# Turned probabilities loaded into every fourth partition, and x loaded ahead of two weight groups

## The chip, the cores and the metric

The kernel runs on one core of a Trainium2 chip. The metric is the time of one execution on the device, in microseconds (us). Five engines work side by side, each through its own instructions in order: TensorE (PE, with its weight loads shown apart as PEld), VectorE (DVE), ScalarE (ACT), GpSimd (POOL) and SyncE (SP). SP issues nearly all transfers here. A transfer is spread over 16 DMA engines; "DMA share" is the mean busy share of these.

## The reference, cut to what matters

```
# attention with a forget gate: 4 batches, 8 heads, 576 positions, head size 64
scores = q @ k.T / sqrt(64) + (cum_i - cum_j)       # cum = cumsum(log(clip(f)))
attn   = softmax(causal(scores));  attn_out = attn @ v
x  = attn_out as (2304 tokens, 512)
h  = maximum(x @ w1_in, 0);        x = (h * h) @ w1_out      # first MLP, 512 -> 2048 -> 512
h  = x @ w2_in;  g = h - tanh(h);  out = g @ w2_out          # second MLP
```

All of it is float32. The kernel gets float32 accuracy out of faster matmuls by splitting an operand into a high and a low part (names ending in h and l, or hi and lo) and adding three products.

## The kernel before, in words

There are 32 units, one for each batch and head. The 8 units of batch 0 are done first; units 8 to 31 then run beside the first MLP, whose matmuls (L159 for `h_step`, L175 for `y_step`) work on tiles of 288 tokens and stand between the attention's matmuls on PE. The MLP of token tile j needs the attention output of these tokens, which goes through the DRAM tensor `x_d` (`store_x`, then `load_x`).

A unit's probabilities `P` stand with queries in the partitions; the product with V wants keys in the partitions. Units 8 to 15 turn them on PE (`trans`). Units 16 to 31 (`UT = 16`) turn them differently: DVE transposes 32x32 blocks into the tile `T` (`turn`), `put` stores T (1 MB) into the DRAM tensor `p_d`, and `get` loads it into the tile `PTl` with four transfers of 256 KB, one for each block b of 32 keys, each into 32 partitions with four runs of 2 KB in a partition. Then POOL rounds `PTl` to `PTh` (`split_p`, L108), DVE leaves the rest in `PTl` (L119), and `pv` multiplies both with V: seven matmuls with 128 rows of weights and 512 to 256 columns (L561), one with the last 64 keys (L558) and one with the first query tile's 64 keys (L563). V comes from `load_v` (tile `VR`), with key 128c + p in partition p.

`T`, `PTl` and `PTh` have one buffer each, so a unit's `get` waits for the product of the unit before, and a unit's first transposition waits for `put` of the unit before. In the loop `attention_late` the pieces of unit k stand between those of unit k - 1 (`split_p`, `pv`); `get(k)` is emitted last.

What sets the order: from MLP tile 2 on (`MARK`) until tile 6, the order of each engine's instructions is chosen when the kernel is built, by a scheduler that works with its own durations of instructions and transfers. Before and after this stretch the order is that of the code.

The second part is the second MLP. `w_load(0, g)` loads the prepared weights of group g (two transfers of 896 KB into tile `wg`), `x_load(b)` the 576 tokens of block b (two transfers of 576 KB into `xa`), and the loop over n makes the steps of 42 matmuls each, eight steps for a token block. Step n works with weight group `HSEQ[n % 8]`, in the order 6, 7, 0, 1, 2, 3, 4, 5; groups 6 and 7 are in place already. In step 3 of a block, `x_op` (ACT, then POOL) begins to split the next block's x. `h_store` stores a step's result `gq` into `g_d`, from SP like the loads.

Of the kernel before, what the change touches and what calls it, by code (L numbers as in the profile page):

```python
# [9 lines left out]
F32 = mybir.dt.float32  # L10
# [22 lines left out]
UT = 16  # L33
# [32 lines left out]
def kernel(  # L66
# [10 lines left out]
    nc = tc.nc  # L77
# [107 lines left out]
    R, QA, QB, VR, VH, ST, XS, P, PT = {}, {}, {}, {}, {}, {}, {}, {}, {}  # L185
# [65 lines left out]

    def load_v(u):
        VR[u] = two.tile([128, 5, D], F32, tag="VR", bufs=2, name="VR")
        nc.sync.dma_start(VR[u], v[u])

    def prep_v(u):
        VH[u] = one.tile([128, 4, 2, D], F32R, tag="VH", name="VH")
# [251 lines left out]
    def turn(t):  # L509
        p, T = P[t], PT["t"]  # L510
        if t == 0:
            nc.vector.transpose(T[0:64, 0:2, 3, 0], p[0:64, :64].rearrange("p (b j) -> p b j", b=2))
            return
        nch = min(t + 1, 4)
        nc.vector.transpose(T[:, :, :nch, t - 1].rearrange("p b a j -> p a b j"),
                            p[:, :nch * 128].rearrange("p (a b j) -> p a b j", a=nch, b=4))
        if t == 4:
            nc.vector.transpose(T[:, 0:2, 2, 0], p[:, 512:576].rearrange("p (b j) -> p b j", b=2))
# [4 lines left out]
    def get(u):  # L523
        src = p_d[u % 2].rearrange("(q i) (b n) -> i q b n", q=4, b=4)
        for b in range(4):
            dst = PT["l"][32 * b:32 * b + 32].rearrange("p q a s j -> p q (a s j)")
            by("get").dma_start(dst.bitcast(F32), src[:, :, b])  # L527

    def split_p(a):
# [6 lines left out]
    def pv(u):  # L536
        vh, vr = VH.pop(u), VR.pop(u)
        b, h = divmod(u, H)
        e = h % 2
        ps = bank(u, "o_ps")  # L540
        if u < UT:
            hi, lo = (PT[k].rearrange("p q a s j -> p (q a s j)").rearrange("p (c t j) -> p c t j", c=4, t=4) for k in "hl")
            po = ps.rearrange("p (s j) -> p s j", s=4)
            at = lambda p, c, t: p[:, c, t:]
            po4, p4 = ps[0:64, 384:512].rearrange("p (q j) -> p q j", q=4), PT["t"][0:64, :, 3, 1]
            po_at = lambda t: po[:, t:]
            p0 = PT["t"][0:64, 2:4, 3, 0]
        else:
            hi, lo = PT["h"], PT["l"]
            po = ps.rearrange("p (q s j) -> p q s j", q=4, s=4)  # L550
            at = lambda p, c, t: p[:, :, c, t:]
            po4, p4 = po[0:64, :, 3], lo[0:64, :, 2, 0].bitcast(F32)
            po_at = lambda t: po[:, :, t:]
            p0 = lo[0:64, 0:2, 3, 0].bitcast(F32)
        seq = [(hi, 0), (hi, 1), (lo, 1), (hi, 2), (lo, 2), (hi, 3), (lo, 3), (None, 4), (lo, 0)]
        for n, (pt, c) in enumerate(seq):
            if pt is None:
                nc.tensor.matmul(po4, vr[0:64, 4], p4, start=False, stop=False)  # L558
                continue
            t = max(0, c - 1)  # L560
            nc.tensor.matmul(po_at(t), vh[:, c].rearrange("p a d -> p (a d)"), at(pt, c, t), start=(n == 0), stop=(n == 8))  # L561
        ps0 = bank(u, "o0_ps")
        nc.tensor.matmul(ps0[0:64, 0:64], vr[0:64, 0], p0, start=True, stop=True)  # L563
        if e == 0:
            XS[0] = two.tile([128, S], F32, tag="xs", name="xs")
        xs = XS[0]
        r = slice(64 * e, 64 * e + 64)
        xt = one.tile([64, 512], F32, tag="xsh", name="xt")
        rounded(nc.scalar, xt, ps[64:128])
        if u < UT:  # L570
            nc.vector.tensor_tensor(xs[r, 64:], ps[0:64], xt, ALU.add)
        else:
            nc.vector.tensor_tensor(
                xs[r, 64:].rearrange("p (s q j) -> p q s j", s=4, q=4),
                ps[0:64].rearrange("p (q s j) -> p q s j", q=4, s=4),
                xt.rearrange("p (q s j) -> p q s j", q=4, s=4), ALU.add,
            )
        rounded(by(pre(u) + "xs0"), xs[r, 0:64], ps0[0:64, 0:64])
        if e == 1:
            store_x(b, h // 2, xs, 0, S)  # L580
# [11 lines left out]
    def attention(u0):  # L592
        for p in range(u0 - 2, UT):
            if u0 - 1 <= p:
                load_v(p + 1)
            for t in (1, 4, 3, 2):
                if p >= u0:
                    trans(p, t)
                    yield
                if u0 <= p + 1:  # L600
                    scores(p + 1, t)
                    if t == 1:
                        scores(p + 1, 0)
                    elif p + 1 == UT:
                        turn(t)
                    yield
                if t == 4 and p + 2 < NU:
                    prep(p + 2)
                if t == 3 and p >= u0:
                    prep_v(p)  # L610
            if p + 3 < NU:
                load(p + 3)
            if p >= u0:
                pv(p)
            if p + 1 == UT:
                turn(1)
                turn(0)
                put(UT)
                get(UT)
            if p >= u0:  # L620
                yield
# [261 lines left out]
    def w_load(s, g):  # L883
        hl = home(s, g)
        for a in range(2):
            nc.sync.dma_start(hl[:, a].bitcast(F32), wg_d[s][g][:, a, s:])
        place(s, g, hl)
# [45 lines left out]
    for g in range(NB * NF + LAG):  # L933
        j, i = divmod(g, NF)
        if (j, i) == MARK:
            first_part = {x.name for x in nc.cur_bb.bb.instructions}
        if j < NB:
# [16 lines left out]
            if j < len(PACE):  # L954
                lo, hi, end = PACE[j]
# [195 lines left out]
    for n in range(NSTEP):  # L1151
        b, g = divmod(n, NG)
        x = [bank2(*RING7[(3 * n + i) % 7])[:, :N2] for i in range(3)]
        BK[n] = [x[0], bank2(0, 0)[:, :N2], x[1], x[2]]
        cp, uv, xc, c22 = (SM[:, 2 * i + n % 2] for i in range(4))
        if n < 3:
            w_load(0, n + 3)
        if g == XLOAD_AT and b + 1 < B:
            x_load(b + 1)
        if n in YGT_AT:  # L1160
            y_load(YGT_AT[n])
        if g == 1 and b:
            x_op(b, ("B22",))

        for p in ("P6", "P1", "P7", "P5"):
            h_prod(n, p)
        nc.scalar.activation(cp, BK[n][0], AF.Copy)
        nc.vector.tensor_tensor(uv, BK[n][1], cp, ALU.add)
        now, end = parts(n)
        for k, a in now:  # L1170
            split_part(k, a)
        for k, a in now:
            for which in range(2):
                prep_store(1, k, which, a, a + 4)
        if b + 1 < B and g in XOP_AT:
            x_op(b + 1, XOP_AT[g])
        if b and g in XOP_NEXT:
            x_op(b, XOP_NEXT[g])
        nc.vector.tensor_tensor(BK[n][2], BK[n][2], uv, ALU.add)
        nc.scalar.activation(xc, BK[n][2], AF.Copy)  # L1180
        if g == NG - 1 and b + 1 < B:
            x_op(b + 1, ("T3",))
        nc.vector.tensor_tensor(c22, BK[n][3], xc, ALU.add)
        nc.vector.tensor_tensor(BK[n][3], BK[n][3], uv, ALU.add)
        if g == NG - 1 and b + 1 < B:
            x_op(b + 1, ("T1",))
        if n in YHI_AT and n == NSTEP - 1:
            y_hi(YHI_AT[n])
        if n:
            GQ[n - 1] = late.tile([128, 4, N2], F32, tag="gq", bufs=2, name="gq")  # L1190
            for k in (0, 3, 1, 2):
                h_rest(n - 1, k)
        if g in TSUM_AT and b + 1 < B:
            x_sum(b + 1, TSUM_AT[g])
        for k in at_step(n, -2):
            raw_wide(k, 0)
        for k in at_step(n, -1):
            raw_wide(k, 1)
        for k in at_step(n, 0):
            for m in range(2):  # L1200
                raw_or(k, m)
            if k + 1 < NG:
                prep_fetch(1, k + 1)
        for d, names in ((1, ("S1", "S3")), (2, ("S2", "S4"))):
            for k in at_step(n, d):
                for name in names:
                    prep_sum(1, k, name)
        for k in at_step(n, -1):
            for m in range(2):
                raw_shift(k, m)  # L1210
        for k, a in end:
            split_part(k, a)
        if n in YSUM_AT:
            y_sum(YSUM_AT[n])
        if n in YHI_AT and n < NSTEP - 1:
            y_hi(YHI_AT[n])
        if n == NSTEP - 2:
            y_lo(0)
        if n:
            h_store(n - 1)  # L1220
        for k, a in end:
            for which in range(2):
                prep_store(1, k, which, a, a + 4)
        if n in YLOAD_AT:
            w_load(1, YLOAD_AT[n])

    n = NSTEP - 1
# [116 lines left out]
```

## Time and profile before

| what | value |
|---|---|
| median of 3 runs | 1060.38 us (1056.74 to 1061.86) |
| the profiled execution: its time | 1054.99 us |
| the profiled execution: its span | 1053.2 us |
| PE busy | 992.8 us (94% of the span) |
| DVE, ACT, POOL busy | 71%, 56%, 38% |
| moved by DMA | 211.55 MB, mean 201 GB/s |

The span runs from the first to the last instruction; the execution's time is 1.8 us longer. All times of instructions below are counted from the span's start. A line number is that of the kernel before. In the profile an idle time stands in front of the instruction that ended it, with what released it behind an arrow.

### The profile page before, as it was taken

The page shows a single profiled execution, that of the slowest core. Times are in us where ns is not written, and L with a number is a line of the kernel's source. Part 1 is how long each engine was busy: PE and PEld are TensorE (multiplying, and loading weights), DVE is VectorE, ACT ScalarE, POOL GpSimd, SP SyncE. Part 2 cuts the span into 40 slices and gives each one's busy share as a digit, 9 for nine tenths or more (in the row PEclk, how much of TensorE's full clock was granted, in tenths as well). Part 3 has the DMA queues.
Part 4 walks back from the last instruction along what each step waited for, and adds up shares of the span by engine and source line. Part 5 has one row for each costly group of instructions (what it writes and reads, how often), then busy time and mean ns, then how long its engine had stood idle before and what let it go on. Part 6 is the DMA issues. An engine that isn't in the chain of part 4 may idle for free.

```text
span 1053.2 us, 19722 instructions
## 1 busy us (share of the span) xinstructions
PE 992.8 (94%) x7008; PEld 927.2 (88%) x7008; DVE 743.7 (71%) x1843; ACT 587.7 (56%) x1314; POOL 400.3 (38%) x484
## 2 busy tenths in 40 slices
PE   4989999999998989898999999979999999999998
PEld 3667678888987979888889999969999999999998
DVE  5897777777876777677733667548787788877851
ACT  5886777665464655545445777526565663333330
POOL 4244455554444344443310555416474630000000
PEclk9999999999998999999999999989999999999999
DMA  8657642224955746755634987786868599535442
GB/s 243 198 151 208 195 153 98 83 82 152 295 165 159 226 159 217 222 139 193 192 97 144 339 320 245 274 320 228 298 241 297 195 352 373 165 95 160 141 147 74
DMA packets 86738, 211.55 MB, mean 201 GB/s; under 512 B 8592, under 2 KB 33232, under 8 KB 84336
## 3 DMA queue, kind: packets, MB, share of 16 engines
q1 hardware_dynamic: 86640, 210.29, 60.3%
q8 instruction: 55, 0.90, 0.4%
q14 instruction: 43, 0.35, 0.1%
HBM read 132.21 MB, written 78.05 MB: 200 GB/s over the span
## 4 chain that ended last, share of the span: by engine, by line
PE 60%; DVE 15%; DMA 15%; ACT 3%; issue 3%; SPq 2%; POOL 1%; POOLq 0%; DVEq 0%; ACTq 0%
PE wp L1085 15%; PE hp L159 11%; PE yp L175 11%; PE wp L1009 10%; DMA PTl<-p_d 6%; PE o_ps L561 3%; DMA p_d<-T 3%; PE wp L1097 2%; PE o_ps L376 2%; DVE PTl L119 2%; DVE P L452 2%; DMA g_d<-gq 2%; DMA xa<-y_d 1%; SPq L527 1%; DVE QA L119 1%
## 5 line engine op out<-in xcount | busy, mean ns | idle before, releaser
L159 PE MATMUL hp<-xhl,w 128*128 128x288 f32 x1536 | 239.4, 302 | 4.8 <-ACT tmp L163 3.9
L159 PEld LDWEIGHTS hp<-xhl,w 128*128 128x128 f32 x1536 | 218.6, 193 | 11.3 <-ACT tmp L163 5.7
L175 PE MATMUL yp<-gh,w 128*128 128x288 f32 x1024 | 196.9, 299 | 0.0
L1009 PE MATMUL wp<-xo,wg 128*128 128x288 f32 x1152 | 161.8, 298 | 8.5 <-DVE gq L1016 8.2
L1009 PEld LDWEIGHTS wp<-xo,wg 128*128 128x128 f32 x1152 | 157.0, 191 | 9.9 <-DVE gq L1016 9.9
L1085 PE MATMUL wp<-go,wg 128*128 128x256 f32 x1344 | 161.4, 283 | 0.0
L1085 PEld LDWEIGHTS wp<-go,wg 128*128 128x128 f32 x1344 | 161.4, 192 | 0.0
L175 PEld LDWEIGHTS yp<-gh,w 128*128 128x128 f32 x1024 | 159.1, 189 | 1.1 <-issue 0.4
L175 PE MATMUL yp<-gl,w 128*128 128x288 f32 x512 | 133.6, 302 | 5.0 <-DVE gl L119 2.5
L163 ACT ACTIVATE tmp<-hp 128x288 f32<-128x288 f32 x128 | 52.0, 407 | 124.6 <-PE hp L159 118.1
L106 ACT ACTIVATE go<-gt 128x1792 fp32r<-128x1792 f32 (+1 forms) x34 | 58.4, 1718 | 101.4 <-PE wp L1085 79.6
L461 ACT ACTIVATE P<-P,ST 128x320 f32<-128x320 f32 (+4 forms) x151 | 84.5, 560 | 43.9 <-DVE ST L452 43.0
L119 DVE TENSOR_TENSOR gl<-tmp,gh 128x288 fp32r<-128x288 f32 x96 | 58.6, 611 | 59.2 <-ACT tmp L165 58.9
L175 PEld LDWEIGHTS yp<-gl,w 128*128 128x128 f32 x512 | 90.6, 191 | 8.7 <-DVE gl L119 4.2
L472 POOL TENSOR_SCALAR P<-P,ST 128x448 f32<-128x448 f32 (+4 forms) x88 | 59.4, 677 | 95.9 <-DVE ST L466 52.2
L119 DVE TENSOR_TENSOR go<-gt,go 128x1792 fp32r<-128x1792 f32 (+1 forms) x34 | 69.6, 2047 | 34.6 <-ACT go L106 31.4
L119 POOL TENSOR_TENSOR wt<-wt,whi 128x512 f32<-128x512 f32 (+1 forms) x48 | 60.0, 1269 | 71.9 <-DVE wt L809 40.2
L452 DVE CUSTOM_DVE_ANT_0 P<-s_ps,mk 128x320 f32<-128x320 f32 (+3 forms) x151 | 63.2, 433 | 26.2 <-PE s_ps L486 14.6
L119 DVE TENSOR_TENSOR PTl<-PTl,PTh 128x512 fp32r<-128x512 f32 (+1 forms) x64 | 51.8, 840 | 37.1 <-POOL PTh L108 37.0
L108 POOL TENSOR_SCALAR PTh<-PTl 128x512 fp32r<-128x512 f32 (+1 forms) x64 | 46.2, 748 | 47.3 <-DMA PTl<-p_d 47.2
L164 ACT ACTIVATE gh<-tmp 128x288 fp32r<-128x288 f32 x128 | 56.7, 443 | 3.3
L165 ACT ACTIVATE tmp<-tmp 128x288 f32<-128x288 f32 x128 | 56.5, 441 | 3.0
(159 smaller groups left out, 1721.8 us busy)
## 6 DMA issues: line engine op xcount, KB each, us to landing
raw<-in_w_dram SPq DMA_DIRECT2D x64, 512.0 KB
wg<-wg_d SPq DMA_DIRECT2D x24, 896.0 KB
g_d<-gq SPq DMA_DIRECT2D x32, 576.0 KB
p_d<-T SPq DMA_DIRECT2D x16, 1024.0 KB
PTl<-p_d SPq DMA_DIRECT2D x64, 256.0 KB
gt<-g_d SPq DMA_DIRECT2D x32, 512.0 KB
R<-in_qk_dram SPq DMA_DIRECT2D x24, 576.0 KB
xhl<-x_d SPq DMA_DIRECT2D x14, 576.0 KB
```

Of the source, the lines that this page charges most:

```text
L106: eng.activation(out, in_, AF.Copy)
L119: eng.tensor_tensor(out, in_, hi.bitcast(F32), ALU.subtract)
L159: nc.tensor.matmul(ps, w[:, k * 128:(k + 1) * 128], x[:, k], start=(jj == 0), stop=(jj == 11))
L163: nc.scalar.activation(tmp, ps, AF.Relu)
L164: nc.scalar.activation(gh, tmp, AF.Square)
L165: nc.scalar.activation(tmp, tmp, AF.Square)
L175: nc.tensor.matmul(yp[m][:, :n], w[:, c], x, start=(at == 0 and j == 0), stop=(at == NF - 1 and j == 2))
L452: nc.vector.tensor_tensor_reduce(p[:rows, a:b], ps[:rows, :b - a], mk[:rows, o:o + b - a], -0.125, 3.0e38 if mn is None else mn, ALU.add, ...
L461: nc.scalar.activation(p[:rows, :n], p[:rows, :n], AF.Exp, bias=mn, scale=-1.0, accum_out=st[:rows, 1, t:t + 1])
L472: by(n_by).tensor_scalar(p[:rows, :n], p[:rows, :n], st[:rows, 3, t:t + 1], 1.0, ALU.mult, ALU.mult)
L1009: nc.tensor.matmul(ps, wg[:, ws, k * 128:(k + 1) * 128], xo[:, xs, k], start=(i == 0 and first_), stop=(i == 5), skip_group_check=True)
L1085: nc.tensor.matmul(ps, wg[:, ws, m * 128:(m + 1) * 128], YO[n][xs][:, YX[xn]], start=(j == 0 and m == 0 and i == 0), stop=(j == 2 and i == ...
```

## The change

First part: `get` places block b into partitions b, b + 4, b + 8, ... (`b::4`) and no longer into 32 neighbours; the values in a partition are in the same order. V of units 16 to 31 is loaded in the same order of keys (key 32b + i of a chunk in partition 4i + b). The last 64 keys and the first tile's 64 keys, which stood in partitions 0 to 63, are now spread over all 128, so that two matmuls of `pv` take 128 rows, half of them zeros; a memset clears a corner of `T` once, before unit 16. Second part: weight groups 3, 4 and 5 are requested one step later each, and group 4 behind `x_load`.

```
 def load_v(u):
-    nc.sync.dma_start(VR[u], v[u])
+    src = v[u] if u < UT else v[u].rearrange("(b i) c d -> i b (c d)", b=4)
+    nc.sync.dma_start(VR[u], src)
 def get(u):
-        dst = PT["l"][32 * b:32 * b + 32].rearrange("p q a s j -> p q (a s j)")
+        dst = PT["l"][b::4].rearrange("p q a s j -> p q (a s j)")
 def pv(u):                                    # u >= UT; rows = 64 for u < UT, else 128
-            po4, p4 = po[0:64, :, 3], lo[0:64, :, 2, 0].bitcast(F32)
+            po4, p4 = po[0:64, :, 3], lo[:, :, 2, 0].bitcast(F32)
-            p0 = lo[0:64, 0:2, 3, 0].bitcast(F32)
+            p0 = lo[:, 0:2, 3, 0].bitcast(F32)
-                nc.tensor.matmul(po4, vr[0:64, 4], p4, start=False, stop=False)
+                nc.tensor.matmul(po4, vr[0:rows, 4], p4, start=False, stop=False)
-        nc.tensor.matmul(ps0[0:64, 0:64], vr[0:64, 0], p0, start=True, stop=True)
+        nc.tensor.matmul(ps0[0:64, 0:64], vr[0:rows, 0], p0, start=True, stop=True)
 def attention(u0):
             if p + 1 == UT:
+                nc.gpsimd.memset(PT["t"][0:64, 2:4, 3, 0], 0.0)
                 turn(1)
 # the loop over n in the second part
-        if n < 3:
-            w_load(0, n + 3)
         if g == XLOAD_AT and b + 1 < B:      # XLOAD_AT = 2
             x_load(b + 1)
+        if 1 <= n < 4:
+            w_load(0, n + 2)
```

The change shows in the order of the instructions at three places. First SP's transfers at the start of the second part, before (`wg` are weight groups, numbered by `wg_d`; `xa` is x, `raw` weights still to be prepared, `g_d` a step's result):

```order
L716 DMA y_d<-yst 128x2x288 x2
L886 DMA wg<-wg_d_2_96 128x1792 x2
L886 DMA wg<-wg_d_3_97 128x1792 x2
L886 DMA wg<-wg_d_4_98 128x1792 x2
L1021 DMA g_d_92<-gq 256x1x576
L886 DMA wg<-wg_d_5_99 128x1792 x2
L901 DMA xa<-y_d 128x2x576 x2
L759 DMA raw<-in_w_dram 128x1024 x2
L1021 DMA g_d_93<-gq 256x1x576
```

And the same place of the changed kernel:

```order
L720 DMA y_d<-yst 128x2x288 x2
L890 DMA wg<-wg_d_2_96 128x1792 x2
L890 DMA wg<-wg_d_3_97 128x1792 x2
L1025 DMA g_d_92<-gq 256x1x576
L905 DMA xa<-y_d 128x2x576 x2
L890 DMA wg<-wg_d_4_98 128x1792 x2
L763 DMA raw<-in_w_dram 128x1024 x2
L1025 DMA g_d_93<-gq 256x1x576
L890 DMA wg<-wg_d_5_99 128x1792 x2
```

Weight groups 4 and 5 stood ahead of x and now stand behind it, group 5 also behind a store. Second, PE at the product of the last unit, 31, before (`o_ps` rows are `pv`; `hp` and `yp` rows are the MLP):

```order
L175 MATMUL yp<-gl,w_1_956 128x288 x4
L561 MATMUL o_ps<-PTh,VH 128x512
L563 MATMUL o_ps<-PTl,VR 64x64
L159 MATMUL hp<-xhl,w_0_1136 128x288 x12
L561 MATMUL o_ps<-PTh,VH 128x512
L175 MATMUL yp<-gh,w_1_1048 128x288 x8
L561 MATMUL o_ps<-PTl,VH 128x512
L561 MATMUL o_ps<-PTh,VH 128x4x96
L561 MATMUL o_ps<-PTl,VH 128x4x96
L561 MATMUL o_ps<-PTh,VH 128x4x64
L175 MATMUL yp<-gl,w_1_1048 128x288 x4
```

And the same product in the changed kernel:

```order
L159 MATMUL hp<-xhl,w_0_1332 128x288 x12
L564 MATMUL o_ps<-PTh,VH 128x512
L566 MATMUL o_ps<-PTl,VR 64x64
L175 MATMUL yp<-gh,w_1_1239 128x288 x8
L564 MATMUL o_ps<-PTh,VH 128x512
L564 MATMUL o_ps<-PTl,VH 128x512
L564 MATMUL o_ps<-PTh,VH 128x4x96
L175 MATMUL yp<-gl,w_1_1239 128x288 x4
L564 MATMUL o_ps<-PTl,VH 128x4x96
L564 MATMUL o_ps<-PTh,VH 128x4x64
L564 MATMUL o_ps<-PTl,VH 128x4x64
```

The whole stretch from unit 16 on is drawn up anew; here the product stands three weight blocks of the MLP later (1332 against 1041 is the block that comes next or just before). Third, POOL before unit 16's store, before and then after:

```order
L119 TENSOR_TENSOR VH<-VR,VH 128x4x64
L119 TENSOR_TENSOR gl<-tmp,gh 128x288
L250 MEMSET ST 128x24
L108 TENSOR_SCALAR xsh<-xs 128x576
L119 TENSOR_TENSOR xs<-xs,xsh 128x576
```

In the changed kernel the same rows are:

```order
L119 TENSOR_TENSOR VH<-VR,VH 128x4x64
L119 TENSOR_TENSOR gl<-tmp,gh 128x288
L619 MEMSET T 64x2x32
L250 MEMSET ST 128x24
L108 TENSOR_SCALAR xsh<-xs 128x576
```

One memset of the corner of T has come in between.

## Rows read from the trace of the kernel before

**Rows 1.** Windows by stage: length, busy time of each engine, granted clock, DMA, GB/s

```profile
250.00:546.00 296.00, 273.79 (x1809) 252.98 (x1809) 213.92 (x646) 152.13 (x388) 125.80 (x163) 0.97 0.61 189
...
676.00:728.00 52.00, 44.24 (x317) 44.01 (x317) 30.01 (x69) 23.34 (x54) 15.21 (x14) 0.90 0.82 309
```

**Rows 2.** Waits from 250 to 546: us in total, times, longest

```profile
PE o_ps L561 <- POOL PTh L108: 13.4, 9, 3.3
...
POOL PTh L108 <- DMA PTl<-p_d: 47.2, 14, 5.5
DVE PTl L119 <- POOL PTh L108: 37.0, 15, 4.5
```

**Rows 3.** Chain that ended last, 250 to 546: one of twelve such pieces

```profile
498.20 5.78 DMA PTl<-p_d
```

**Rows 4.** Timeline of SP and POOL around one `put` and `get`: start, length

```profile
307.74 0.33 SPq L521 DMA_DIRECT2D p_d<-T  x1
311.91 1.75 SPq L527 DMA_DIRECT2D PTl<-p_d  x4
...
319.27 2.69 POOL L108 TENSOR_SCALAR PTh<-PTl 128x512 fp32r<-128x512 f32 x4 [2.90 <-DMA PTl<-p_d]
```

**Rows 5.** Windows: while T is stored, while PTl is loaded, and at L1266

```profile
308.60:311.10 2.50, 2.50 (x21) 2.50 (x21) 2.08 (x10) 2.34 (x7) 0.12 (x1) 1.00 1.02 424
313.00:318.00 5.00, 4.31 (x33) 4.08 (x32) 4.24 (x20) 2.76 (x10) 1.72 (x2) 1.00 0.99 229
...
1020.00:1024.00 4.00, 4.00 (x35) 4.00 (x35) 0.81 (x2) 2.27 (x2) 0.00 (x0) 1.00 0.93 311
```

**Rows 6.** Timeline of SP at L1266: start, length

```profile
1017.51 9.36 SPq L1266 DMA_DIRECT2D a<-wg_d  x16
```

**Rows 7.** Waits of PE's weight loads from 250 to 546, and weight loads by form

```profile
PEld o_ps L563 <- issue: 4.3, 17, 0.4
PEld o_ps L561 <- issue: 2.7, 16, 0.2
...
L498 PEld LDWEIGHTS t_ps<-ident,P 128*64 128x64 f32 x8 | 0.9, 110 | 0.0
L499 PEld LDWEIGHTS t_ps<-ident,P 64*64 64x64 f32 x8 | 0.8, 106 | 1.6 <-issue 1.6
```

**Rows 8.** Windows inside a stretch of half clock and after it

```profile
336.40:339.40 3.00, 3.00 (x13) 2.90 (x13) 3.00 (x13) 0.00 (x0) 3.00 (x4) 0.50 0.01 3
344.40:347.40 3.00, 3.00 (x25) 3.00 (x24) 1.77 (x9) 2.68 (x7) 1.39 (x2) 1.00 0.92 381
```

**Rows 9.** Timeline around the last unit's product and the next token tile

```profile
543.50 0.50 PE L561 MATMUL o_ps<-PTl,VH 128*128 128x512 f32 x1
...
548.23 1.95 SPq L726 DMA_DIRECT2D xhl<-x_d  x2
...
568.34 1.86 PE L159 MATMUL hp<-xhl,w 128*128 128x288 f32 x12 [0.50 <-ACT tmp L163]
```

**Rows 10.** Timeline of SP, ACT and PE at the start of the second part

```profile
675.35 4.33 SPq L886 DMA_DIRECT2D wg<-wg_d  x6
...
685.96 0.94 SPq L901 DMA_DIRECT2D xa<-y_d  x2
...
701.44 0.68 ACT L106 ACTIVATE xo<-xa 128x576 fp32r<-128x576 f32 x1 [10.59 <-DMA xa<-y_d]
...
674.25 8.14 PE L1009 MATMUL wp<-xo,wg 128*128 128x288 f32 x60
...
694.23 1.76 PE L1009 MATMUL wp<-xo,wg 128*128 128x288 f32 x12
703.75 5.45 PE L1009 MATMUL wp<-xo,wg 128*128 128x288 f32 x24 [7.76 <-DVE gq L1016]
...
709.83 4.96 PE L1009 MATMUL wp<-xo,wg 128*128 128x288 f32 x36
```

**Rows 11.** Window while weights and x queue up

```profile
666.00:686.00 20.00, 20.00 (x153) 20.00 (x152) 8.43 (x19) 8.76 (x20) 4.94 (x4) 1.00 0.99 388
```

More of the change, by code (lines that the diff above doesn't have):

```diff
@@ L544, in pv @@
             at = lambda p, c, t: p[:, c, t:]
+            rows = 64
             po4, p4 = ps[0:64, 384:512].rearrange("p (q j) -> p q j", q=4), PT["t"][0:64, :, 3, 1]
@@ L551, in pv @@
             at = lambda p, c, t: p[:, :, c, t:]
-            po4, p4 = po[0:64, :, 3], lo[0:64, :, 2, 0].bitcast(F32)
+            rows = 128
+            po4, p4 = po[0:64, :, 3], lo[:, :, 2, 0].bitcast(F32)
             po_at = lambda t: po[:, :, t:]
-            p0 = lo[0:64, 0:2, 3, 0].bitcast(F32)
+            p0 = lo[:, 0:2, 3, 0].bitcast(F32)
         seq = [(hi, 0), (hi, 1), (lo, 1), (hi, 2), (lo, 2), (hi, 3), (lo, 3), (None, 4), (lo, 0)]
```

## The prediction, made before the changed kernel ran

> **What bounds the kernel now.** I read the windows by stage first, then PE's waits in the stages where PE isn't full, then the chain, and last the timelines there. PE is the engine to watch: it is busy 94% of the span, so a change pays only where PE is idle or slow. Two places have both, and they are the two that the change touches. From 250 to 546 us, where units 16 to 31 run beside the MLP, PE is busy 273.8 of 296 us, so 22.2 idle, at a mean granted clock of 0.97; from 676 to 728, the start of the second part, it is busy 44.2 of 52 us at 0.90 [rows 1]. In the first place the largest wait of PE is for PTh, 13.4 us in nine waits; POOL, which makes PTh, waits 47.2 us for the loads of PTl, and DVE 37.0 for POOL [rows 2]. The chain shows twelve such loads, of 5.8 us and the like [rows 3]. In the second place PE has one wait of 7.76 us; behind it stands ACT's wait of 10.59 us for x [rows 10].
>
> **First part: the load.** What is moved is the same: 64 transfers of 256 KB, four for a unit, 1.05 MB. Today they go at 229 GB/s with the DMA engines busy 0.99 of the time, while T, the same bytes, is stored at 424 GB/s with them as busy [rows 5]. So the transfers aren't short of requests; each is slow. 1.05 MB takes 4.6 us at 229 GB/s and 2.5 at 424. The change spreads each transfer over all 128 partitions, where it now fills 32 neighbours. The store's runs are 8 KB long, the load's 2 KB; runs of 1 KB, the loads of L1266 (128 KB each, to 128 partitions), go at 311 GB/s [rows 5, 6], which would be 3.4 us. [...] Between 311 and 424 I take 380 GB/s: 2.8 us, 1.8 saved. Issue is no limit: four take 1.75 us on SP, and from the first issue to POOL's start it is 7.4 us now [rows 4].
>
> [...]
>
> What it is worth on PE: nine waits of 13.4 us in all, 1.5 in the mean, the longest 3.3. With 1.8 less each, the longest keeps 1.5 and the others about nothing: 12 us gained (0 if the load isn't faster, up to all 22.2 if the other waits, which partly stand behind DVE's wait for PTh, go too). The loads are also in a ring: a unit's load waits for the product before, and DVE can't turn the next unit while it waits for PTh. So the gain isn't given back at once: two units take about 37 us now (296 us for 16), and PE's own work in them is 34 (273.8 for 16), so with two loads shorter by 1.8 the ring gets to 33.4 and PE's own work is late next.
>
> **First part: the rest.** The two matmuls with 64 rows become 128 rows of the same columns. PE's weight loads now stand for 4.3 us ahead of L563 and 2.7 ahead of the L561 that follow L558, released by nothing but issue. The forms elsewhere say why: 64*64 loads (L499) have 1.6 us of such idle time in eight, 128*64 loads (L498) none, and at about the same length [rows 7]. So up to 7.0 us go; PE itself feels less, since its matmuls overlap. I take half, 3.5 us (0 to 7). The memset is one short instruction on POOL ahead of unit 16's store, in POOL's idle time there; nothing. V's load in another order has the same number of runs and bytes; nothing.
>
> [...]
>
> All orders from unit 16 on are drawn up anew, by a scheduler that doesn't go by this trace. What counts is the room between a unit's last product and the next unit's first: the matmuls between them in the two orders, at 0.134 us each (24 in 3.2 us, below), are 6.5 to 15 us before and 7 to 14.5 after. No place got tighter than the tightest was. The last unit's product stands later by three weight blocks, against token tile 6, which begins 568.3 - 543.5 = 24.8 us after that product now, while x is requested after 4.7 us [rows 9]; the order now leaves 132 matmuls, some 17.6 us, which still covers the request and a load of the length in [rows 3].
>
> **Second part.** x is requested at 685.96, behind six groups of two transfers, and ACT gets it at 701.44; ACT had nothing to do for 10.59 us, so it was ready at 690.85 [rows 10]. In this stretch the transfers go at 388 GB/s with the DMA engines full [rows 11], one after the other. Two groups less ahead of x are 4 x 0.918 MB = 3.67 MB, 9.5 us: x is there at about 692. ACT then loses 1.1 us; PE ran on for 5.1 us after ACT stopped (to 696.0), so it doesn't notice. PE gets back 7.76 us, and what follows the wait too: 24 matmuls took 5.45 us after it, where 36 take 4.96 later [rows 10], so 3.3 would do (3.2 without the last one's tail); 2.1 us. Together 9.9 us. What the moved loads cost: group 4 lands behind x, at about 692 + 4.7 = 697; group 5 is behind as many bytes as x was, plus 1.05 MB of `raw` and a store of 0.59 MB, so at about 701.4 + 4.2 = 706. They are needed in steps 6 and 7; at 42 matmuls, 5.6 us, a step, these begin 34 and 39 us after the part's first matmul at 674.3 [rows 10], so at 708 and 713. The margins are 11 and 7 us.
>
> **Sum.** 12 + 3.5 + 4 + 9.9 = 29.4 us. The profiled execution took 1055.0; that gives 1025.6. The median of the runs stands 5.4 us above that execution, so I forecast 1031 us.
>
> **Rivals.** First: the scheduler's order eats the gain. The single buffers of T, PTl and PTh remain, and DVE waits 37 us for POOL; if the new order puts turns behind waits, the first part gives a third, 6.5 of 19.5 us. For it: PE's other waits are small and many. Against: PE's work is longer than the shortened ring. Time 1060.4 - 16.4 = 1044.
>
> Second: the load isn't faster, since its rate comes from its size or from 2 KB runs. For it: no row shows 32 scattered partitions. Against: 128 KB transfers in 1 KB runs go at 311 GB/s [rows 5, 6]. Then only the second part and some of the 3.5 remain: 1060.4 - 11 = 1049. [...]
>
> [...]
>
> **Chances.** Forecast 0.64, first rival 0.20, second 0.11, third 0.05. About 0.5%, 5.3 us, can be told from no change. Faster by more: all of the forecast and nearly all of the first two rivals, 0.91; same 0.05; slower 0.04. Range: with every term of the first part at its upper bound the time would be 1013; not all come together, so 1018; with the second part alone it is 1050. So 1018 to 1050, which leaves the third rival and the edges out; the forecast's own range is 1020 to 1040.
>
> **What would show it.** Right: windows of a load at 350 GB/s or more; the time from the first load's issue to POOL's PTh under 6 us; PE's waits for PTh under 3 us in all; no idle time by issue ahead of the L563 matmuls; ACT's wait for x at about 1 us and no PE wait near 700; PE busy over 98% there. Wrong: a rate that stays near 229, PE idle over 15 us in the first stage, or PE waiting for weights in steps 6 and 7 of the second part.

## The result

| | median, us (lowest to highest) | runs | ratio to before, 95% |
|---|---|---|---|
| before, same set | 1061.12 (1056.74 to 1061.98) | 4 | |
| changed kernel | 1032.32 (1029.46 to 1036.73) | 4 | 0.974 (0.970 to 0.979) |
| before, a later set | 1057.13 (1052.32 to 1061.13) | 11 | |
| changed kernel again | 1033.07 (1026.90 to 1036.06) | 6 | 0.9773 (0.9742 to 0.9803) |

The change makes the kernel 2 to 3% faster. The runs of the changed kernel lie 7 and 9 us apart within a set (those of the kernel before up to 11), and the two executions of the changed kernel that were profiled happen to be the ends: 1036.73 us (span 1034.9), the slowest of its four, and 1026.90 (span 1025.1), the fastest of its six. Both are used below, as the first and the second profile, since a term of a few us can't be sized from one alone.

**By stage.** The answer to [rows 1]: windows of the first profile from 250 to 546 us, and 52 us from just behind the second part's first matmul (columns: length, busy time of PE, PE's weight loads, DVE, ACT and POOL, granted clock, DMA share, GB/s).

```profile
250.00:546.00 296.00, 279.97 (x1918) 261.50 (x1918) 217.81 (x656) 158.76 (x406) 131.22 (x167) 0.99 0.56 194
...
662.75:714.75 52.00, 49.30 (x361) 47.88 (x359) 36.95 (x75) 25.60 (x62) 20.45 (x18) 1.00 0.87 333
```

And the same two of the second profile:

```profile
250.00:546.00 296.00, 283.20 (x1961) 265.39 (x1960) 216.27 (x652) 160.91 (x411) 130.23 (x166) 0.99 0.59 202
...
656.30:708.30 52.00, 50.83 (x379) 50.23 (x378) 37.41 (x82) 28.49 (x66) 22.54 (x19) 1.00 0.88 337
```

In the first stage PE does 109 or 152 more matmuls in the same 296 us, at a clock of 0.99 for 0.97; in the second it is busy 49.3 or 50.8 of 52 us for 44.2, at a clock of 1.00 for 0.90. The line of the second part's first product (matmuls, ns, first and last start) gives the border of the two parts, in the first and then in the second profile:

```profile
L1013 PE MATMUL wp<-xo,wg x1152: 288/295/402, 661.0 to 845.7; 128*128 128x288 f32 x192
```

```profile
L1013 PE MATMUL wp<-xo,wg x1152: 288/294/403, 654.6 to 835.9; 128*128 128x288 f32 x192
```

Before, that matmul starts at 674.25 [rows 10] and the span goes on for 378.9 us. So the first part gave 13.2 us in the one profile and 19.6 in the other, and the second part, now 373.9 and 370.5 us long, 5.0 and 8.4.

**The load.** The answer to [rows 4] in the first profile, the same unit (start, length, what was waited for):

```profile
309.65 0.32 SPq L522 DMA_DIRECT2D p_d<-T  x1
313.54 2.53 SPq L528 DMA_DIRECT2D PTl<-p_d  x4
...
319.77 1.21 POOL L108 TENSOR_SCALAR PTh<-PTl 128x512 fp32r<-128x512 f32 x2 [1.05 <-DMA PTl<-p_d]
```

The window of that load, as in [rows 5]:

```profile
315.00:319.00 4.00, 3.22 (x24) 2.99 (x24) 3.81 (x15) 2.44 (x8) 2.18 (x3) 1.00 0.76 265
```

From the first issue to POOL it is 6.23 us, 1.13 less. The DMA engines are no longer full: 265 GB/s at a share of 0.76, where it was 229 at 0.99. But SP now needs 2.53 us to issue the four, not 1.75: a quarter of the partitions with a stride of four takes 0.63 us to issue, 32 neighbours took 0.44.

This unit flatters the change. In another one the load got no shorter, before and then after:

```profile
421.82 1.74 SPq L527 DMA_DIRECT2D PTl<-p_d  x4
429.13 2.92 POOL L108 TENSOR_SCALAR PTh<-PTl 128x512 fp32r<-128x512 f32 x4 [5.54 <-DMA PTl<-p_d]
```

```profile
419.16 2.53 SPq L528 DMA_DIRECT2D PTl<-p_d  x4
427.30 2.91 POOL L108 TENSOR_SCALAR PTh<-PTl 128x512 fp32r<-128x512 f32 x4 [4.43 <-DMA PTl<-p_d]
```

Here it is 7.31 us before and 8.14 after. Over the 14 loads for which POOL waits, the time from first issue to POOL is 7.4 us before (median; 7.2 to 8.0) and 7.1 in the first profile (5.6 to 8.1) or 6.6 in the second (6.1 to 8.2). In windows from 1.5 us after the first issue to 1 us before POOL's start, the medians are 231 GB/s at a share of 0.95 before and 263 at 0.83 in the first profile. So the typical load is 0.4 to 0.8 us shorter.

The waits that answer to [rows 2], in the first profile:

```profile
POOL PTh L108 <- DMA PTl<-p_d: 38.4, 14, 5.8
DVE PTl L119 <- POOL PTh L108: 24.5, 15, 3.8
...
PE o_ps L564 <- POOL PTh L108: 8.0, 7, 2.7
```

PE's wait fell from 13.4 to 8.0 us (6.0 in the second profile). The waits ahead of the weight loads, which answer to [rows 7], did not fall:

```profile
PEld o_ps L566 <- issue: 4.3, 17, 0.4
PEld o_ps L564 <- issue: 2.9, 17, 0.2
```

**The second part.** Its start in the timeline of the first profile, the answer to [rows 10]:

```profile
671.57 1.82 SPq L905 DMA_DIRECT2D xa<-y_d  x2
673.43 1.25 SPq L890 DMA_DIRECT2D wg<-wg_d  x2
...
677.83 0.81 SPq L763 DMA_DIRECT2D raw<-in_w_dram  x2
678.74 0.55 SPq L1025 DMA_DIRECT2D g_d<-gq  x1
678.91 0.69 ACT L106 ACTIVATE xo<-xa 128x576 fp32r<-128x576 f32 x1 [1.29 <-DMA xa<-y_d]
...
689.34 1.19 DVE L1020 TENSOR_TENSOR gq<-wp,sm 128x288 f32<-128x288 f32 x3 [3.54 <-DMA g_d<-gq]
...
689.85 3.46 PE L1013 MATMUL wp<-xo,wg 128*128 128x288 f32 x24 [1.49 <-DVE gq L1020]
```

ACT's wait for x is 1.29 us, for 10.59 before. There is a new wait, and the chain names it (start, length):

```profile
678.74 10.51 DMA g_d<-gq
```

The store of step 1's result is issued behind x, weight group 4 and `raw`, and takes 10.51 us to land. There are two result buffers, so step 3 must wait for it: DVE 3.54 us, PE 1.49. In the second profile DVE waits 2.95 us there and PE 0.90.

### The profile page after: what moved, and what is told of

The parts are those of the page before. It is cut to its first block, busy times and chain, and to the rows that moved or that the text cites. A ratio compares the mean times of both kernels' runs of the same rounds, so it can differ in the third digit from the quotient of the medians.

```text
span 1034.9 us, 19719 instructions
## 1 busy us (share of the span) xinstructions
PE 985.8 (95%) x7008; PEld 921.4 (89%) x7008; DVE 747.2 (72%) x1843; ACT 586.4 (57%) x1314; POOL 402.4 (39%) x485
## 4 chain that ended last, share of the span: by engine, by line
PE 65%; DVE 14%; DMA 11%; ACT 5%; issue 3%; SPq 2%; POOL 1%; DVEq 0%; POOLq 0%; ACTq 0%
PE wp L1089 16%; PE yp L175 12%; PE hp L159 12%; PE wp L1013 12%; DMA PTl<-p_d 4%; PE o_ps L564 3%; DMA p_d<-T 2%; PE wp L1101 2%; DMA g_d<-gq 2%; PE o_ps L377 2%; DVE PTl L119 2%; DVE P L453 1%; DMA raw<-in_w_dram 1%; PE s_ps L486 1%; DVE QA L119 1%
## 5 line engine op out<-in xcount | busy, mean ns | idle before, releaser
L159 PE MATMUL hp<-xhl,w 128*128 128x288 f32 x1536 | 235.9, 299 | 6.2 <-ACT tmp L163 5.5
L159 PEld LDWEIGHTS hp<-xhl,w 128*128 128x128 f32 x1536 | 214.5, 189 | 12.4 <-ACT tmp L163 7.1
L175 PE MATMUL yp<-gh,w 128*128 128x288 f32 x1024 | 199.3, 300 | 0.0
L119 DVE TENSOR_TENSOR PTl<-PTl,PTh 128x512 fp32r<-128x512 f32 (+1 forms) x64 | 49.4, 801 | 24.5 <-POOL PTh L108 24.5
```

Of the source, the lines that this page charges most:

```text
L119: eng.tensor_tensor(out, in_, hi.bitcast(F32), ALU.subtract)
L159: nc.tensor.matmul(ps, w[:, k * 128:(k + 1) * 128], x[:, k], start=(jj == 0), stop=(jj == 11))
L175: nc.tensor.matmul(yp[m][:, :n], w[:, c], x, start=(at == 0 and j == 0), stop=(at == NF - 1 and j == 2))
```

## The experiments

Each set of four was timed beside the kernel before on the same chip, in five rounds; its median was 1059.27, 1056.91 and 1057.13 us in the three sets, so kernels of different sets are compared by their ratios.

| set | kernel | median us | ratio, 95% | second part starts (profile) | PE busy until then |
|---|---|---|---|---|---|
| | before | | | 674.3 | 626.3 |
| 1 | first part alone | 1041.13 | 0.9828 (0.9807 to 0.9850) | 657.8 | 618.2 |
| 1 | second part alone | 1051.79 | 0.9936 (0.9913 to 0.9958) | 676.1 | 626.3 |
| 1 | one load, own order | 1032.25 | 0.9752 (0.9730 to 0.9775) | 659.3 | 619.9 |
| 1 | changed, old order | 1046.65 | 0.9884 (0.9850 to 0.9919) | 670.9 | 626.1 |
| 2 | old load, new order | 1043.53 | 0.9872 (0.9837 to 0.9907) | 667.8 | 621.7 |
| 2 | one load, new order | 1026.04 | 0.9710 (0.9673 to 0.9747) | 652.5 | 618.5 |
| 2 | groups behind stores | 1034.44 | 0.9793 (0.9756 to 0.9829) | 658.0 | |
| 2 | full width, own order | 1036.28 | 0.9809 (0.9775 to 0.9842) | 661.2 | |
| 3 | changed, again | 1033.07 | 0.9773 (0.9742 to 0.9803) | 654.6 | 616.2 |
| 3 | full width, new order | 1030.34 | 0.9750 (0.9723 to 0.9776) | 656.5 | |
| 3 | one load, x, then store | 1024.75 | 0.9703 (0.9678 to 0.9727) | 650.4 | |
| 3 | the same and full width | 1024.84 | 0.9695 (0.9670 to 0.9720) | 651.2 | |

"New order" is the order of every engine's instructions that the scheduler made for the changed kernel, "old order" the one for the kernel before, "own order" what it made for that kernel.

**Which part gave what.** The first part alone keeps the old loop of the second part:

```
-        if g == XLOAD_AT and b + 1 < B:
-            x_load(b + 1)
-        if 1 <= n < 4:
-            w_load(0, n + 2)
+        if n < 3:
+            w_load(0, n + 3)
+        if g == XLOAD_AT and b + 1 < B:
+            x_load(b + 1)
```

> The edit of the first part alone (strided load, v in the same order); the order of loads in the second part is that of the kernel before. By the profiles of the changed kernel and of the one before, the first part gave 13.2 us and the second 5.1. Theory 1, that the two edits add up and the profiled execution of the changed kernel was an ordinary one: 13 to 15 us faster than before, some 1047 us, and the second part's wait for x of about 10 us on ACT is back. Theory 2, that nearly all of the 28.8 us between the medians belongs to the first part: 1037 us or less. In both the first matmul of the second part comes 12 to 15 us earlier than before and waits of POOL for the loads at the changed kernel's length (first issue to PTh 5.6 to 7.3 us).

Measured: 18.1 us below before in its set (1.72%, interval 1.5 to 1.9), between the two theories. The second alone is the kernel before with these lines the other way round.

> The edit of the second part alone; the first part as before. Theory 1, that the wait for the store of a result buffer takes back part of the gain: 5 us faster than before, some 1056 us, the wait for x on ACT gone (1 to 2 us left of 10.6), and a wait of PE of 1 to 2 us near the fourth step that the kernel before does not have. Theory 2, that the second part gives the 9.9 us that were forecast when the first part is not changed: 1051 us and no such wait. Theory 3, that loads only change places: within 3 us of before.

Measured: 7.5 us by the medians, 6.8 by the ratio (0.64%, 0.42 to 0.87). Its PE waits 1.19 us for gq at 704.58, so the wait for the store is there without the first part too. The time lies between theories 1 and 2. The two ratios add up to 2.4% (25 us), and the changed kernel has 2.3 to 2.6. The parts don't help or hinder each other measurably. Four profiles have the changed kernel's first part unaltered (both of the changed kernel, the first part alone, and the groups behind stores below), and in them the second part starts at 654.6 to 661.0 us; in the two with the old first part it starts at 674.3 and 676.1. So the first part's gain is well outside what one profile moves.

**Load or order.** To keep the order, the kernel's body is scheduled once with the other load, and the order that came out is forced on each engine:

```
+    middle = [by_name[n] for n in order[1] if n in by_name and n not in first_part and n in second_part]
-    for chain in ([by_name[n] for n in order if n in first_part], ...
+    for chain in ([by_name[n] for n in order[0] if n in first_part], middle, ...
```

> The changed kernel with every engine's instructions of the first part in the order of the kernel before (the one memset that was added stands where it stood); only the load, v's order and the rows of the product are changed, and the second part is as in the changed kernel. Theory 1, that the faster load itself gives the first part's gain: within 4 us of the changed kernel. Theory 2, that the scheduler's new order eats part of the load's gain: 5 to 12 us under the changed kernel, near 1022 us. Theory 3, that the new order is itself the gain, since a load only 1 us faster in 16 products cannot give 13 us through the waits alone: 6 us or more over the changed kernel, and PE's waits for PTh between 8 and 13 us.

> The converse of the run with the old order: load into contiguous partitions, v and the 64-row matmuls as in the kernel before, but every engine's instructions of the first part in the order of the changed kernel; second part as changed. With the two loads and the two orders this closes a table of four, all with the new second part: old load and old order 1051.8 us, new load and old order 1046.6, new load and new order 1032.3. Theory A, the new order is worth some 14 us by itself, whatever the load takes: 1036 to 1040 us. Theory B, the order pays only with the faster load, since it asks for the turned probabilities at the time at which the scheduler took the faster load to land: 1046 us or more, with more waiting of PE for PTh than the changed kernel's 8.0 us in 7 waits and half-clock stretches back to four or more between 240 and 560. Theory C, the order cannot be had with the old load without a loss: over 1052 us.

Measured against the second part alone (0.9936, old load and old order): the new load in the old order 0.9884, the old load in the new order 0.9872, both new 0.974 and 0.9773. So each alone is worth 0.5 to 0.6%, some 6 us, and both 17 to 21 us. Whether the rest, 5 to 9 us, is more than the two added can't be told: each ratio is uncertain by 0.35%. In the run with the old order theory 3 came nearest (14 us over the changed kernel, 11.9 us of waits for PTh). In its converse the time lies between theories A and B: the order is worth something with the old load, but not 14 us.

The table shows that they save different things, since the same 4128 matmuls run until the second part starts. The load alone leaves PE's busy time as it was (626.1 for 626.3) and takes 3.2 us of its 48.0 idle. The order alone takes 4.5 us of busy time and 2.0 idle. Both take 6.7 busy and 6.5 idle in the first profile, 10.1 and 9.6 in the second. Most of the busy time that goes is the clock. What the granted clock falls short of 1.00, summed over windows of 1 us until the second part starts, is 10.2 us before, 11.9 with the load alone, 6.8 with the order alone, and 5.1 and 1.7 with both: 3.4 us less with the order alone, 5.1 and 8.5 less with both. The other profiles agree: in the three with the old order the clock is at about 0.50 for 20 to 24 us of this time, in the nine with the new order for 3 to 17. The first-stage windows of the new load in the old order, then of the old load in the new order:

```profile
250.00:546.00 296.00, 277.50 (x1839) 257.15 (x1838) 216.13 (x647) 154.76 (x395) 127.97 (x166) 0.96 0.56 191
```

```profile
250.00:546.00 296.00, 275.26 (x1865) 255.77 (x1864) 215.30 (x652) 155.38 (x397) 129.58 (x165) 0.98 0.62 189
```

The clock is 0.96 in the one and 0.98 in the other, though PE waits for PTh about as long in both (11.9 and 11.3 us). What is different stands ahead of the falls. The new load in the old order (length, PE busy, clock, DMA share, GB/s):

```profile
317.00:322.20 5.20, 3.32 (x20) 1.00 0.86 327
322.30:325.70 3.40, 3.39 (x13) 0.52 0.04 12
...
331.00:336.00 5.00, 3.43 (x24) 1.00 0.73 228
336.00:339.30 3.30, 3.30 (x15) 0.52 0.01 2
```

The old load in the new order, the same two places:

```profile
317.00:322.20 5.20, 4.08 (x28) 1.00 1.05 299
322.30:325.70 3.40, 3.37 (x21) 1.00 0.42 173
...
331.00:336.00 5.00, 4.05 (x27) 1.00 0.63 182
336.00:339.30 3.30, 3.30 (x26) 1.00 0.00 0
```

In the old order PE was busy 3.3 and 3.4 us ahead of each of these, and the clock was 0.52 in the windows behind it, with 13 and 15 matmuls. In the new order PE was busy 4.1 us there, and the clock stayed at 1.00: 21 and 26. Not every such stretch is followed by a fall (in the new order PE is busy 2.76 us from 450 to 455 at 1.00, and 12 matmuls take 1.74 us at 457.76, where 12 took 1.75 at 450.06), so this is what these places show and no rule.

**Is the load limited by its issue?** The four transfers as one over all 128 partitions, to the same addresses:

```
-        src = p_d[u % 2].rearrange("(q i) (b n) -> i q b n", q=4, b=4)
-        for b in range(4):
-            dst = PT["l"][b::4].rearrange("p q a s j -> p q (a s j)")
-            by("get").dma_start(dst.bitcast(F32), src[:, :, b])
+        src = p_d[u % 2].rearrange("(q i) n -> q (i n)", q=4)
+        src = src.rearrange("q (p m) -> p q m", m=512)
+        dst = PT["l"].rearrange("p q a s j -> p q (a s j)")
+        by("get").dma_start(dst.bitcast(F32), src)
```

> The changed kernel with one transfer over all 128 partitions in place of the four, to the same addresses (partition 4i+b takes piece b of row i in each). Issue theory, that the load's length is now set by the issue of four strided transfers at 0.6 us each: SP is busy with one issue of 0.4 to 0.8 us instead of 2.5, first issue to PTh falls from 5.6-7.3 us to 4 to 5, PE's waits for PTh fall from 8.0 to under 4 us in 240 to 545, and the time is 3 to 8 us under the changed kernel. Engine theory, that the 16 DMA engines need the time for 1 MB wherever it is issued: first issue to PTh stays within 0.5 us and the time within 2 us. Third possibility: one transfer has its packets laid on fewer engines or makes them later, first issue to PTh over 7.5 us, and the time is 5 us or more over the changed kernel.

PE's waits for PTh fell to 2.6 us, as the issue theory had it, and the time did not fall. But the scheduler had made a third order for it. So the same load was run in the new order:

> The changed kernel with one transfer over all partitions for the four, and every engine's instructions of the first part in the order of the changed kernel (one load of x on SP stands one place later), so that nothing but the load's length differs. With an order of its own the one transfer gave 1032.25 us, no gain, though PE waited for PTh only 2.6 us in place of 8.0. Theory A, what the shorter load saves in waits is not on the path that decides: 1031 to 1034 us. Theory B, the shorter load is worth its waits and the order that the scheduler made for it took them back: 1026 to 1029 us.

Measured 0.9710 of before, against 0.974 and 0.9773 of the changed kernel in other sets. The comparison in one set is that of the kernel with one load in the new order and a moved store (below): 0.9703 (0.9678 to 0.9727) beside 0.9773 (0.9742 to 0.9803), 8.3 us by the medians. By the profiles none of this is the store's: the second part is no shorter with it moved. So theory B is borne out: the shorter load pays. That the order made for it took this back is read from ratios of different sets, 0.9752 against 0.9710 and 0.9703. The timeline of the one load in the new order, same unit as above:

```profile
310.34 0.33 SPq L524 DMA_DIRECT2D p_d<-T  x1
314.22 0.37 SPq L530 DMA_DIRECT2D PTl<-p_d  x1
...
319.58 1.40 POOL L110 TENSOR_SCALAR PTh<-PTl 128x512 fp32r<-128x512 f32 x2 [0.17 <-DMA PTl<-p_d]
```

Its window, and its waits in the first stage:

```profile
315.50:318.50 3.00, 2.29 (x18) 2.06 (x16) 2.94 (x10) 2.60 (x9) 1.91 (x2) 1.00 0.92 329
```

```profile
POOL PTh L110 <- DMA PTl<-p_d: 21.7, 10, 4.1
DVE PTl L121 <- POOL PTh L110: 11.4, 11, 2.5
...
PE o_ps L572 <- POOL PTh L110: 2.3, 2, 1.7
```

One issue takes 0.37 us for 2.53; from issue to POOL it is 5.36 us, for 6.23 with four strided and 7.36 with four neighbouring transfers; the DMA engines are busy again, at a share of 0.92, and move 329 GB/s. Over the ten loads for which POOL waits the median from issue to POOL is 5.8 us. So one transfer in place of four is what shortens the load. Whether this is the shorter issue on SP or the larger size of the transfer isn't shown, since both change together.

**The wait for the store.** In the changed kernel, groups 3 to 5 behind the store of their step:

```
-        if 1 <= n < 4:
-            w_load(0, n + 2)
...
             h_store(n - 1)
+        if 1 <= n < 4:
+            w_load(0, n + 2)
```

> The changed kernel with the loads of weight groups 3, 4 and 5 issued behind the store of the step before in steps 1, 2 and 3, not ahead of it; nothing else. Theory A, that the wait of PE for gq of 3.0 us in 4 comes from the store of step 1, which landed 10.51 us after its issue behind weight groups: these waits fall under 1 us, the store lands within 6 us of its issue, and the time is 2 to 3 us under the changed kernel, 1029 to 1030 us. Theory B, that the steps there are short of DVE and ACT anyway: waits of the same sum in other names and a time within 1 us of the changed kernel. Theory C, the groups come late: PE waits for wg, 2 us or more over the changed kernel.

DVE's waits for the store went, and the time is no less than the changed kernel's: 0.9793 (0.9756 to 0.9829). x now stands behind group 3 and is late again, as ACT shows to DVE and DVE to PE (DVE, then PE, in that run's timeline):

```profile
680.53 0.46 DVE L1185 TENSOR_TENSOR sm<-wp,sm 128x288 f32<-128x288 f32 x1 [4.88 <-ACT sm L1182]
...
681.77 4.97 PE L1013 MATMUL wp<-xo,wg 128*128 128x288 f32 x24 [2.07 <-DVE gq L1020]
```

So one load took another's place. Theory B came nearest, with a time no better and waits of 3.9 us in place of 3.0, but the late x was in none. The second try, together with the one load in the new order, leaves group 3 and x where they were and moves only groups 4 and 5:

```
-        if 1 <= n < 4:
-            w_load(0, n + 2)
+        if n == 1:
+            w_load(0, 3)
...
             h_store(n - 1)
+        if n in (2, 3):
+            w_load(0, n + 2)
```

> One transfer for the load, in the changed kernel's order, and in the second part x first, then the store of step 1, then weight group 4, the store of step 2 and group 5: x is not put behind a group as in the run with all groups behind stores, and the store of step 1 has one group less ahead of it. Theory A, the shorter load (3 to 6 us) and the wait for the store (2 to 3 us) add up: 5 to 9 us under the changed kernel, waits of PE for gq under 1.5 us in the second part. Theory B, the wait for the store only changes its name: 3 to 6 us under, as with the one load alone, 0.971 of the kernel before.

Theory B: 0.9703, where the one load alone had 0.9710. At the start of the second part DVE's wait for the store fell from 4.1 us (with the one load alone) to 1.6. But later stores make up for it: over the whole second part DVE waits 6.5 us for stores, where it was 6.1, and PE 3.9 us for gq, where it was 3.2. The second part is 375.3 us long, no shorter than before this edit (375.0).

**The waits ahead of the narrow weight load.** The last matmul of each product gets a weight tile as wide as its neighbours':

```
-        nc.tensor.matmul(ps0[0:64, 0:64], vr[0:rows, 0], p0, start=True, stop=True)
+        nc.tensor.matmul(ps0[:, 0:64], vr[0:rows, 0:2].rearrange("p a d -> p (a d)"), p0, start=True, stop=True)
```

> The changed kernel with 128 columns of v for the last matmul of each product (the 64 of the piece wanted and the 64 of the next one, whose result rows nobody reads), so that its weight tile is 128*128 like that of its neighbours, in place of 128*64; nothing else. Theory A, that the waits ahead of this weight load (4.3 us in 17, ended by issue) come from the change of the tile's width between neighbours: they go, and the time falls by 2 to 4 us if PE decides there. Theory B, that they come from the change between float32 and the rounded type: they stay, and the time is within 1 us of the changed kernel. Theory C, that the wider load itself takes longer than the wait: 1 to 3 us over the changed kernel.

> The full-width weight load for the last matmul of each product as before, now with every engine's instructions of the first part in the order of the changed kernel. In the earlier run the waits ahead of this load fell from 4.3 us to 0.2, but the scheduler had made another order and the time did not fall. Theory A, the waits were on the path and the other order hid it: 2 to 4 us under the changed kernel. Theory B, PE's clock of work does not feel them (the matmuls before are still running while the load waits, and the wider load runs 261 ns a pass in place of 246): within 1.5 us of the changed kernel. Theory C, the wider load costs more: over 1.5 us above it.

The waits ahead of this load go in both runs. In the one with the new order only this is left:

```profile
PEld o_ps L565 <- issue: 2.9, 17, 0.2
PEld o_ps L562 <- issue: 0.6, 4, 0.2
PEld o_ps L570 <- issue: 0.2, 1, 0.2
```

L570 is the load in question: 4.3 us became 0.2. So this wait hangs on the tile's width, as theory A of the first text had it, and not on the type, which stayed. Width alone doesn't make such a wait, though: L562, with a tile of 128*64 between the same neighbours, waits 0.6 us in four, and the load of 128*128 behind it still waits (L565, 2.9 us in 17). What else it takes stays open. The time: 0.9750 beside 0.9773 in the same set, 2.7 us by the medians, with intervals that overlap. On top of the one load it was tried again:

> The same with the full-width weight load for the last matmul of each product, same order. If that load saves its waits, 2 to 4 us under the run with the one transfer and the moved store; if PE does not feel them, within 1.5 us of it.

1024.84 us beside 1024.75. So the time doesn't feel these 4 us, or by less than these runs can tell. (In its own order the full width was no faster either, 0.9809; there the order had changed too.)

**Control.**

> The changed kernel once more, unaltered, beside the three kernels that are to be compared with it. All theories: 0.974 of the kernel before, as first measured, between 0.970 and 0.979; its profile shows how far the first matmul of the second part (661.0 us in the first profile, 658.0 in a kernel with the same first part) moves from one execution to another.

0.9773, inside what was expected, and the second part started 6.4 us earlier than in the first profile: as much as several of the terms in dispute.

## Why the prediction was right, and where its steps were not

The forecast of 1031 us is 1.3 below the median. Its sum was 29.4 us from one profile of before to one of after. The two profiles of the changed kernel give 18.3 and 28.1, so the sum was at the upper end. That the first part came to 18.1 us alone, of 19.5 forecast, is luck: the load gave less than half of its term, and an order that the sum had at nothing filled the gap. The signs that the prediction named for being right say so. Only the one on x held: ACT's wait is 1.29 and 1.34 us. The load's rate (265 GB/s in the window shown, for 350), its time to POOL (6.23 us there, for under 6), PE's waits for PTh (8.0 and 6.0 us, for under 3) and the idle time ahead of the weight loads (4.3 us, for none) did not come. One sign of being wrong did, in the first profile: PE was idle 16.0 us in the first stage, where over 15 was to count against it (12.8 in the second).

- **The load, 12 us: the step that failed is the 1.8 us saved on each load, and with it "Issue is no limit".** The load got 1.13 us shorter in the unit shown and 0.4 to 0.8 by the medians, and issuing the four went from 1.75 to 2.53 us. As one transfer it is 2.0 us shorter in the unit shown and 1.6 by the medians. Alone, in four transfers, in the old order, the load gave 5.5 us (0.9936 to 0.9884, intervals that just overlap), not 12. PE's waits for PTh were to fall under 3 us; they fell to 8.0 and 6.0. One transfer for the four has them at 2.3, so the prediction's sign can be met, though not by the changed kernel.
- **What the load is limited by.** The windows say that scattering over all partitions helps: 229 GB/s at a share of 0.99 became 265 at 0.76, so while a DMA engine is busy it moves 1.5 times as much (349 for 231; over all 14 loads the median is 1.3 times, 325 for 251). The second rival, that the rate comes from the size or from the 2 KB runs, falls as it stands: size and runs are the same and the rate isn't. In time it is half right, since the load gets little shorter. No run here times one of the four transfers by itself, as four are always under way together.
- **The rows, 3.5 us: failed.** The prediction read the forms as if 64 rows made the wait, since 128*64 loads of the transposes had none. Those stand among their like; the last load of the product waits 0.25 us, at 128 rows as at 64, and stops when its tile is as wide as its neighbours'. And even where the wait is gone, no gain can be measured.
- **The 4 us in the sum, for the clock, are a term that no run shows.** What the runs showed in its place: PE's busy time for the same matmuls fell by 6.7 and 10.1 us, 5.1 and 8.5 of it by the clock. It isn't the shorter load that does it: with the load alone the clock falls 11.9 us short, for 10.2 before, and with the order alone 6.8, which is 3.4 us gained.
- **The order, counted as nothing.** The prediction looked at the room between products and found no place tighter; the first rival had the order lose 13 us. In fact the new order gained some 6.8 us with the old load (0.9936 to 0.9872). That an order can lose shows elsewhere: with the one load, the scheduler's own order has 0.9752 and starts the second part at 659.3, the changed kernel's order 0.9710 and 652.5. Whether it loses by the rival's mechanism, turns behind waits, isn't shown.
- **The second part, 9.9 us: mechanism right, size too large.** x comes in time (1.29 us of wait on ACT, forecast 1.1), and PE doesn't wait for weights; but it is busy 95 and 98% of the 52 us, where over 98 was forecast. It gave 5.0 and 8.4 us by the profiles and 6.8 alone. The step that was missing is the store behind the moved loads: group 4 was priced for when it lands, not for what it delays, and step 3 waits for the buffer of step 1 (PE 1.49 and 0.90 us). That this wait makes up the whole shortfall isn't shown: both tries to remove it brought other waits and no gain.
- **The offset of 5.4 us** between the profiled execution of before and the median was rightly kept: without it the same sum gives 1025.6. It is chance which run gets profiled, as the two profiles of the changed kernel show.
- **A slower kernel,** given 0.04, is out: the scattered form moves more in each busy us (349 GB/s for 231 in the windows shown), not less.

What stays open: why the scheduler's order for one load is worse than the order for four; why the second part is 370 to 372 us long in some executions and 374 to 375 in others, with the waits for gq larger in the latter (1.6 us in the second profile, 3.0 in the first); which of issue and size limits the four transfers; and whether load and order together give more than their sum.

## What to carry to other kernels

Where a scheduler draws the order anew, run the old data path in the new order and the new one in the old before a gain is put down to the edit: here the order alone gave about as much as the load alone. A strided quarter of the partitions took longer to issue than a block (0.63 us for 0.44), so if the addresses allow it make it one transfer over all of them: that made the fastest versions here, 1025 to 1026 us, 0.7% under the changed kernel. And when a load is moved ahead of another, price the store that now queues behind it, through the buffer that the store holds. Last, size a load over all its repetitions and not by one: the unit shown first here saved 1.13 us, the median 0.4 to 0.8.

## What the runs showed of the hardware

- SP issued a transfer to 32 neighbouring partitions in 0.44 us, one to every fourth partition in 0.63, one to all 128 (1.05 MB) in 0.37. The first two have the same bytes and the same source, and differ in the stride of the destination's partitions alone.
- One weight load of 128*64 among loads of 128*128 waited 0.25 us, and nearly nothing when it was made 128*128 (4.3 us in 17 against 0.2). Another of 128*64 in the same product hardly waited (0.5 us in three).
- The mean granted clock over the same 296 us was 0.96 to 0.97 or 0.98 to 0.99, depending on how the same instructions were ordered, with PE's largest wait nearly the same (11.9 and 11.3 us).
